# Chunked attention and a two-layer block on one core: direct first v, half-row scores, PSUM seeds, three more quarters by sevens, a written order

## The chip, the core and the metric

One core of a Trainium2 chip. The metric is device time in microseconds from the start to the end of one execution. The runs of the kernel before took 275.38, 275.7 and 276.49 us; their median, 275.7 us, is the time before. The profiled execution has its own time: its span, from the first to the last instruction, is 273.8 us. TensorE multiplies, VectorE and ScalarE work on tiles and take results out of PSUM (eight banks), GpSimd works on tiles and issues the loads, SyncE issues the transposing transfers and the stores.

## The reference

Attention inside chunks of 64 rows over q, k, v of 8 x 8 heads x 576 rows x 64, all float32:

```python
scores = scale * np.matmul(q_c, k_c.transpose(0, 1, 2, 4, 3))
scores = scores - np.max(scores, axis=-1, keepdims=True)
attn = np.exp(scores)
attn = attn / (np.sum(attn, axis=-1, keepdims=True) + 1e-09)
out = np.matmul(attn, v_c)
```

The result, with heads side by side, is x of 4608 tokens x 512. Two layers follow: `h = x @ w_in` (512 x 2048), `g = max(0.01 h, h)`, `g @ w_out` (2048 x 512), float32 out. The kernel works in float16 with sums in float32.

## The kernel before

**Groups.** Attention runs in 36 groups `u` of 128 tokens (two chunks of all eight heads). A group's steps, by the names they have in the program (`group`, line 865): `arrive` loads q and k (GpSimd's queue, converted to float16 on the way); `pe_t` transposes q and k on TensorE for u < 10 (`stage_tq`, `stage_tk`: the tiles qp and kp, four matmuls each), later groups by SyncE's transposing transfers `t`; `p` copies q into QZ (two copies, one for each half of the heads, into a tile whose other half is zero, so that one 128-row matmul gives two heads' scores); `k` copies kp to KT; `s` makes the scores in eight matmuls of 64 moving columns (`stage_s`, line 446, tile Sp); `m`, `b`, `x`, `z`, `n` are maximum, subtraction, exponential, sum with 1e-9 added and reciprocal, and scaling (tiles mx, sh, ex, z/ze/zi, en); `e` and `d2` transpose en on TensorE and copy it (tpe, et), or `d` does it by a transfer; `v` multiplies by v in eight matmuls (`stage_v`, tile xp), and `a` copies xp to xT, the input of the first layer.

**v.** v lies in VB as 128-row tiles whose two diagonal 64 x 64 blocks hold two heads and whose other blocks are zero (steps `zv`). From the second batch on, `load_v` (line 110) loads it straight into place in two transfers, one for each 64-row half. The first batch comes in five transfers of 128 token rows each into spare tiles (`load_v_rows`, line 124), and 18 copies on ScalarE, VectorE and GpSimd put it in place (`place_v`, line 129).

**Layers.** Tokens are cut into four blocks of 128 and eight of 512 (`BLOCKS`), j = 0 to 11. The first four, and blocks 4 and 5 in the first layer, are plain: `mm1` (tile hT) with 128 moving columns, `g` the leaky ReLU on ScalarE, `mm2` (oP), `out`, `save`. In blocks 6 to 11 a "quarter" of the first layer can be made by seven products in place of eight (`first_fast`, line 996, tiles hA, hB, hC; `FAST`, line 53, tells how many of the four quarters, `UNIT` whether the unit is 256 or 512 tokens). There, product 1 goes to PSUM bank A; a ScalarE copy `d` seeds bank B with it, product 2 adds to B; products 6, 7 and 4 add to A, with copies `u2` and `u3` taken between; 5 and 3 go to C; VectorE adds `+u3` and `+u2`; four leaky ReLUs finish it. The second layer of blocks 4 to 11 is made in the same way (`second_fast`, line 1055, tiles oA, oB, oC, fourteen half-products `m2` of eight matmuls with 256 columns), but there `d` copies product 1 to SBUF, product 2 opens bank B by itself, and VectorE adds the two into the output's C11 part. The sums of g that the products need are `sf`, those of x are `xf`, those of the weights `wf` and `vf`.

**Order.** All steps are put in a list with costs, and `run` (line 637) orders them: a list scheduler with a model of engines and load queues picks the next step, banks and spare tiles, with several hundred small adjustments in `TUNE` (line 776) and the engine of many steps in `ON` (line 820). Before a late step of the start it puts `idle` matmuls on the identity (line 532). Each engine executes its instructions in the order emitted, and so does each queue: GpSimd's carries all loads. The start's load order stands in `front` (line 826): q and k of group 1, k of 2, w_in's first quarter (Q0, two halves), the identity, q2, q3, v's first three pieces, k3, Q1, Q2, and so on; w_out comes in four parts P0 to P3.

Of the kernel before, what the change touches and what calls it, by code (L numbers as in the profile page):

```python
# [16 lines left out]
def kernel(  # L17
# [15 lines left out]
    CH = 64  # L33
# [19 lines left out]
    FAST = {6: 4, 7: 3, 8: 4, 9: 2, 10: 4, 11: 4}  # L53
    UNIT = {6: 256, 7: 256}
    POOL_N, POOL_X, POOL_S = 9, 20, 20
# [66 lines left out]
    V_T: dict[int, bass.AP] = {}  # L122

    def load_v_rows(n):
        r0, r1 = n * G, min((n + 1) * G, S)
        V_T[n] = sbp.tile([128, H, D], FP16, name="v_t", tag=f"tmp{(2 + n) % 6}", bufs=1)
        nc.gpsimd.dma_start(out=V_T[n][:r1 - r0], in_=v[0, :, r0:r1, :].rearrange("h p d -> p h d"))
# [67 lines left out]
    def leaky(to, of):  # L195
        nc.scalar.activation(out=to, in_=of, func=AFT.Prelu, bias=0.0, scale=1.0, alpha=0.01)  # L196

    def copy(to, of):
        nc.scalar.activation(out=to, in_=of, func=AFT.Copy, bias=0.0, scale=1.0)  # L199
# [23 lines left out]
    def evict2(j, ti):  # L223
        OSB[j, ti] = osb_tile()[:, 0]
        copy(OSB[j, ti], OP.pop((j, ti)))
# [52 lines left out]
    def x_form(j, h, i):  # L278
        (x11, x12), (x21, x22) = x_halves(j, h)
        f = x_sums(j, h)  # L280

        def less(to, a, b):
            (nc.gpsimd if j >= POOL_X else nc.vector).tensor_tensor(out=to, in0=a, in1=b, op=ALU.subtract)
# [53 lines left out]
    def g_form(j, i):  # L337
# [5 lines left out]
        if i == 0:  # L343
            plus(SF[j, 0], a21, a22)
        elif i == 1:
            minus(SF[j, 1], SF[j, 0], a11)
        elif i == 2:
            (nc.gpsimd if j >= POOL_S else nc.vector).tensor_tensor(out=a21, in0=a11, in1=a21, op=ALU.subtract)
        else:
            (nc.gpsimd if j >= POOL_S else nc.vector).tensor_tensor(out=a12, in0=a12, in1=SF[j, 1], op=ALU.subtract)  # L350

    def out_product(j, m, p, tag=None):
# [6 lines left out]
        }[m]  # L359
        if j == LAST:  # L360
            key = (j, p, "o" + IN[m])
            if m in OPENS:
                PA[key] = bank([128, HM], "o" + IN[m], tag)
            to, fresh = PA[key], m in OPENS
        else:
            key = (j, "o" + IN[m])
            if m in OPENS and p == 0:
                PA[key] = bank([128, 2, HM], "o" + IN[m], tag)
            to, fresh = PA[key][:, p, :], m in OPENS and p == 0
# [46 lines left out]
    def stage_k(u):  # L416
        KT[u] = sbp.tile([128, 4, 2, CH], FP16, name="KT", tag="KT", bufs=4)
        nc.scalar.activation(out=KT[u], in_=KP.pop(u), func=AFT.Copy, bias=0.0, scale=1.0)
# [27 lines left out]
    def stage_s(u, tag="Sp"):  # L446
        qz, kt = QZ[u % NQZ], KT.pop(u)
        Sp = psp.tile([128, 8, CH], FP32, name="Sp", tag=tag, bufs=1)
        for i in range(8):
# [19 lines left out]
    def stage_x(u):  # L469
        E[u] = sbp.tile([128, 8, CH], FP16, name="ex", tag="ex", bufs=2)  # L470
        nc.scalar.activation(out=E[u], in_=SH.pop(u), func=AFT.Exp, bias=0.0, scale=SCL)  # L471

    ZI: dict[int, bass.AP] = {}

    def stage_z(u):
        z = sbp.tile([128, 8], FP32, name="z", tag="z", bufs=2)
        nc.vector.tensor_reduce(out=z, in_=E[u], axis=AXL.X, op=ALU.add)  # L477
        ze = sbp.tile([128, 8], FP32, name="ze", tag="ze", bufs=2)
        nc.vector.tensor_scalar_add(out=ze, in0=z, scalar1=1e-9)
        ZI[u] = sbp.tile([128, 8], FP32, name="zi", tag="zi", bufs=2)  # L480
        nc.vector.reciprocal(out=ZI[u], in_=ze)  # L481
# [45 lines left out]
    def stage_a(u):  # L527
        xp = XP.pop(u)
        at = u * G % RING
        nc.scalar.activation(out=xT[:, :, at:at + G], in_=xp, func=AFT.Copy, bias=0.0, scale=1.0)  # L530
# [26 lines left out]
    class Hold:  # L557
# [3 lines left out]
        def fits(self, slots):  # L561
            return [y for y in slots if not self.written or y[1] in written]

    written: set = set()

    class Step:
# [12 lines left out]
    free: dict[str, list[tuple[float, object]]] = {  # L579
        "bank": [(0.0, x) for x in BANKS], "tmp": [(0.0, x) for x in range(NTMP)],  # L580
    }

    class Queues:

        def __init__(self):
            self.now, self.ring, self.out, self.n = 0.0, ([], []), ({}, {}), [0, 0]
            self.done, self.still = 0, []  # L590

        def matmuls(self, n, t):
            self.done += n
            if self.done >= 140:
                self.done -= 128
                if t > STALLS_FROM:
                    self.still.append((t + 0.75, t + 0.75 + STALL))

        def put(self, q, step, at, packets, slow):
            self.ring[q].append([at, packets, slow, step])  # L600
            self.n[q] += 1

        def heads(self):
            return [r[0] if r and r[0][0] <= self.now + 1e-9 else None for r in self.ring]

        def rates(self, h):
            if any(a - 1e-9 <= self.now < b - 1e-9 for a, b in self.still):
                return (0.0, 0.0)
            if h[0] and h[1]:
                return (370.0, 695.0 / h[1][2]) if h[1][2] > 1 else (425.0, 399.0)  # L610
            return (ALONE[0] if h[0] else 0.0, ALONE[1] / h[1][2] if h[1] else 0.0)

        def event(self):
            h = self.heads()
            v = self.rates(h)
            t = [self.now + x[1] / y for x, y in zip(h, v) if x and y]
            t += [r[0][0] for r, x in zip(self.ring, h) if r and not x]
            if any(h):
                self.still = [x for x in self.still if x[1] > self.now + 1e-9]
                t += [y for x in self.still for y in x if y > self.now + 1e-9]  # L620
            return min(t, default=None)

        def advance(self, to, landed):
            while self.now < to:
                e = self.event()
                t = to if e is None else min(e, to)
                h = self.heads()
                for x, y in zip(h, self.rates(h)):
                    if x:
                        x[1] -= (t - self.now) * y  # L630
                self.now = t
                for q, x in enumerate(h):
                    if x and x[1] < 1e-6:
                        self.ring[q].pop(0)
                        landed(q, x[3], t + (AFTER[q] if q == 0 or self.ring[0] else 2.0))

    def run():
        now = {e: 0.0 for e in LAT}
        now.update(pe=3.8, act=2.6, dve=0.95, pool=1.2, sp=1.3)
        left = {id(s): len(s.after) for s in steps}  # L640
        users: dict[int, list[Step]] = {}
        for s in steps:
            for x in s.after:
# [590 lines left out]
```

## Time and profile before

| | us |
|---|---|
| median of three runs (275.38 to 276.49) | 275.7 |
| span of the profiled execution | 273.8 |
| TensorE busy (PE), 96% of the span | 263.2 |
| weight loads (PEld, beside PE) | 238.2 |
| VectorE (DVE) | 208.2 |
| ScalarE (ACT) | 193.9 |
| GpSimd (POOL) | 158.9 |
| first matmul / first product of the first layer (hT) starts | 5.96 / 18.35 |

A row of the chain or of the view in order of time gives the start, the length, the engine, the line of the program, what is written from what, and a count. The length of a TensorE row runs to the last result; the distance to the next row's start is what the row costs the queue. In the stages, each pair is an engine's busy time and its instruction count. The granted TensorE clock is 1.00 in all stages.

### The profile page before, as it was taken

The page shows a single profiled execution, that of the slowest core. Times are in us where ns is not written, and L with a number is a line of the kernel's source. Part 1 is how long each engine was busy: PE and PEld are TensorE (multiplying, and loading weights), DVE is VectorE, ACT ScalarE, POOL GpSimd, SP SyncE. Part 2 cuts the span into 40 slices and gives each one's busy share as a digit, 9 for nine tenths or more (in the row PEclk, how much of TensorE's full clock was granted, in tenths as well). Part 3 has the DMA queues.
Part 4 walks back from the last instruction along what each step waited for, and adds up shares of the span by engine and source line. Part 5 has one row for each costly group of instructions (what it writes and reads, how often), then busy time and mean ns, then how long its engine had stood idle before and what let it go on. Part 6 is the DMA issues. An engine that isn't in the chain of part 4 may idle for free.

```text
span 273.8 us, 8229 instructions
## 1 busy us (share of the span) xinstructions
PE 263.2 (96%) x3406; PEld 238.2 (87%) x3406; DVE 208.2 (76%) x375; ACT 193.9 (71%) x359; POOL 158.9 (58%) x198
## 2 busy tenths in 40 slices
PE   1999999999999999999999999999999999999995
PEld 1889578799999999999999999899999989888884
DVE  5895285789978898899788999897879865831671
ACT  6588947778475644999796369978866896378721
POOL 8999783967898959587758778657351000000000
PEclk9999999999999999999999999999999999999999
DMA  9999999999999999999999999999954100220233
GB/s 134 154 191 183 182 176 176 155 173 217 151 158 152 120 143 208 170 144 234 154 155 121 136 140 247 133 186 197 136 84 151 43 19 2 77 79 0 79 115 116
DMA packets 162004, 38.27 MB, mean 140 GB/s; under 512 B 153008, under 2 KB 157616, under 8 KB 161968
## 3 DMA queue, kind: packets, MB, share of 16 engines
q0 software_dynamic: 114384, 18.09, 97.0%
q1 hardware_dynamic: 46544, 19.41, 42.2%
q8 instruction: 26, 0.43, 0.6%
q10 hardware_dynamic: 1040, 0.26, 0.4%
q14 instruction: 10, 0.08, 0.2%
HBM read 36.70 MB, written 9.44 MB: 169 GB/s over the span
## 4 chain that ended last, share of the span: by engine, by line
PE 90%; ACT 3%; DMA 3%; POOL 2%; issue 1%; DVE 0%; POOLq 0%
PE oA L371 20%; PE hT L185 17%; PE hA L323 14%; PE oC L371 10%; PE hC L323 7%; PE oP L210 5%; PE oB L371 5%; PE hB L323 3%; PE Sp L451 3%; PE xp L517 3%; DMA q_in<-in_q_dram 3%; PE tpe L495 1%; PE idle L535 1%; ACT gT L196 1%; ACT xT L530 1%; PE qp L404 1%
## 5 line engine op out<-in xcount | busy, mean ns | idle before, releaser
L371 PEld LDWEIGHTS <-gT 128*128 128x128 f16 x640 | 61.1, 98 | 6.6
L185 PE MATMUL hT<-xT,w_inT 128*128 128x128 f16 (+1 forms) x864 | 58.6, 225 | 0.1
L185 PEld LDWEIGHTS <-w_inT 128*128 128x128 f16 x864 | 53.1, 98 | 2.0 <-issue 0.4
L444 POOL COPY QZ<-QT 64x512 f16<-64x512 f16 x52 | 36.6, 705 | 20.0 <-DMA QT<-q_in 13.1
L196 ACT ACTIVATE gT<-hT 128x512 f16<-128x512 f32 x60 | 35.1, 599 | 15.9 <-PE hT L185 15.6
L235 DVE TENSOR_TENSOR tmp<-hC,tmp 128x512 f32<-128x512 f32 x42 | 27.9, 678 | 16.6 <-PE hC L323 8.3
L487 POOL TENSOR_TENSOR en<-ex,zi 128x512 f16<-128x512 f16 x22 | 23.8, 1083 | 26.8 <-DVE zi L481 12.3
L323 PEld LDWEIGHTS <-VF 128*128 128x128 f16 x448 | 34.5, 98 | 2.4
L93 POOL DMA_DIRECT2D q_in<-in_q_dram x39 | 33.8, 871 | 4.5 <-DMA w_outT<-in_moe_w_out_dram 1.8
L93 POOL DMA_DIRECT2D k_in<-in_k_dram x39 | 33.5, 863 | 1.2 <-DMA VB<-in_v_dram 0.8
L461 DVE TENSOR_REDUCE mx<-Sp 128x8 f32<-128x512 f32 x36 | 24.6, 684 | 10.3 <-PE Sp L451 10.2
L371 PE MATMUL oA<-WF,gT 128*128 128x256 f16 x256 | 32.2, 273 | 0.0
L199 ACT ACTIVATE tmp<-hA 128x512 f32<-128x512 f32 x42 | 24.3, 602 | 6.8 <-PE hA L323 6.8
L196 ACT ACTIVATE gT<-tmp 128x512 f16<-128x512 f32 x42 | 26.4, 634 | 3.7 <-DVE tmp L235 3.6
L323 PEld LDWEIGHTS <-w_inT 128*128 128x128 f16 x336 | 26.2, 98 | 1.9
L471 ACT ACTIVATE ex<-sh 128x512 f16<-128x512 f32 x36 | 22.8, 633 | 7.0 <-DVE sh L465 6.8
L371 PEld LDWEIGHTS <-S 128*128 128x128 f16 x256 | 24.6, 98 | 2.8
L477 DVE TENSOR_REDUCE z<-ex 128x8 f32<-128x512 f16 x36 | 24.3, 676 | 3.3 <-ACT ex L471 3.2
L530 ACT ACTIVATE xT<-xp 128x512 f16<-128x512 f32 x36 | 21.4, 597 | 7.6 <-PE xp L517 7.4
L465 DVE TENSOR_TENSOR sh<-Sp,mx 128x512 f32<-128x512 f32 x36 | 24.5, 681 | 0.6
L323 PE MATMUL hA<-XF,VF 128*128 128x128 f16 (+1 forms) x224 | 24.7, 246 | 0.0
L199 ACT ACTIVATE tmp<-oA 128x512 f32<-128x512 f32 (+1 forms) x27 | 14.9, 552 | 11.7 <-PE oA L371 11.6
(76 smaller groups left out, 478.7 us busy)
## 6 DMA issues: line engine op xcount, KB each, us to landing
out_dram<-osb SPq DMA_DIRECT2D x14, 512.0 KB, 5.2
VB<-in_v_dram POOLq DMA_DIRECT2D x14, 288.0 KB, 9.1
q_in<-in_q_dram POOLq DMA_DIRECT2D x31, 128.0 KB, 8.3
k_in<-in_k_dram POOLq DMA_DIRECT2D x31, 128.0 KB, 8.4
w_inT<-in_moe_w_in_dram POOLq DMA_DIRECT2D x8, 256.0 KB, 7.5
w_outT<-in_moe_w_out_dram POOLq DMA_DIRECT2D x4, 512.0 KB, 9.0
out_dram<-osb SPq DMA_DIRECT2D x6, 256.0 KB, 5.5
v_t<-in_v_dram POOLq DMA_DIRECT2D x4, 128.0 KB, 7.0
```

The costliest lines, as they stand in the source:

```text
L93: nc.gpsimd.dma_start(out=t[a - u * G:z - u * G], in_=src[b, :, r:r + z - a, :].rearrange("h p d -> p h d"))
L185: nc.tensor.matmul(out=hT[:, i, :], lhsT=w_inT[:, t, fc * 128:(fc + 1) * 128], rhs=xT[:, t, r0 % RING:r0 % RING + tb], start=(i == 0 and t ...
L196: nc.scalar.activation(out=to, in_=of, func=AFT.Prelu, bias=0.0, scale=1.0, alpha=0.01)
L199: nc.scalar.activation(out=to, in_=of, func=AFT.Copy, bias=0.0, scale=1.0)
L235: (nc.vector if e == "dve" else nc.gpsimd).tensor_tensor(out=to, in0=a, in1=b, op=ALU.add)
L323: nc.tensor.matmul(out=PA[key][:, c, :], lhsT=w[:, t, fc * 128:(fc + 1) * 128], rhs=x[:, t, :], start=(m in (1, 5) and c == 0 and t == 0), ...
L371: nc.tensor.matmul(out=to, lhsT=lhs[:, fc, p * 128:(p + 1) * 128], rhs=rhs[:, fc, :], start=(fresh and fc == 0), stop=(fc == HB - 1), skip ...
L444: nc.gpsimd.tensor_copy(out=QZ[u % NQZ][part, :, :, s, :], in_=QT[u][part].rearrange("p i (e t) -> p i e t", e=2))
L461: nc.vector.tensor_reduce(out=MX[u], in_=SP[u], axis=AXL.X, op=ALU.max)
L465: nc.vector.tensor_tensor(out=SH[u], in0=SP.pop(u), in1=MX.pop(u).unsqueeze(2).to_broadcast((128, 8, CH)), op=ALU.subtract)
L477: nc.vector.tensor_reduce(out=z, in_=E[u], axis=AXL.X, op=ALU.add)
L530: nc.scalar.activation(out=xT[:, :, at:at + G], in_=xp, func=AFT.Copy, bias=0.0, scale=1.0)
```

## The change

1. `load_v_rows` and `place_v` go; the first batch of v is loaded by `load_v`, straight in place, in four pieces of two or three chunks, two transfers each, and the load order of the start is another.
2. The scores of groups 0 to 3 (`SQ = 4`) are made by sixteen matmuls, each on one 64-row half, from an unpadded copy of q (one copy, `stage_q1`), not from QZ.
3. `second_fast`: `d` copies product 1 into PSUM bank B, product 2 adds to it, and the new step `c11` copies the sum out.
4. `FAST` is 4 in all six blocks: 24 quarters by sevens, not 21 (one more in block 7, two in block 9).
5. The sum's tail is cut in steps (`z`, `ze`, `zi`), and many steps may run on another engine (`ON`): 21 of the 36 `ze` on ScalarE, five of the `a`, and some copies and leaky ReLUs on VectorE; some `xf` and one `sf` on GpSimd.
6. The scheduler, its queue model and `TUNE` go. `ORDER` lists all 1459 steps by number, with the bank or spare tile of each and the number of idle matmuls before it.

```diff
-    FAST = {6: 4, 7: 3, 8: 4, 9: 2, 10: 4, 11: 4}
+    FAST = {6: 4, 7: 4, 8: 4, 9: 4, 10: 4, 11: 4}
...
+    SQ = 4
...
-    def place_v(c, m, e):
-        to = VB[0][m * CH:(m + 1) * CH, :, c, m * CH:(m + 1) * CH]
-        of = V_T[c // 2][c % 2 * CH:(c % 2 + 1) * CH, m * H // 2:(m + 1) * H // 2, :]
-        move(e, to, of)
...
+    def stage_q1(u, e):
+        QT[u] = sbp.tile([128, H // 2, 128], FP16, name="QT", tag="QT", bufs=4)
+        move(e, QT[u], QP.pop(u).rearrange("p i e t -> p i (e t)"))
...
+        if u < SQ:
+            qt = QT.pop(u)
+            for i in range(8):
+                g, e, m = i // 4, i // 2 % 2, i % 2
+                for s in range(2):
+                    half = slice(s * CH, (s + 1) * CH)
+                    nc.tensor.matmul(
+                        out=Sp[half, i, :], lhsT=qt[half, 2 * m + g, e * CH:(e + 1) * CH], rhs=kt[half, 2 * m + g, e, :],
+                        start=(i == 0), stop=True, skip_group_check=True,
+                    )
+            return
...
+        for i, fill, *slots in ORDER:
+            s = steps[i]
+            if fill:
+                idle(fill[0], BANKS[fill[1]])
+            for h, slot in zip(s.take, slots):
+                h.slot = BANKS[slot] if h.pool == "bank" else slot
             s.emit()
...
-        for what in "q1 k1 k2 Q0 I q2 q3 V0 V1 V2 k3 Q1 Q2 q5 V3 q4 P0 k5 P1 k4 q6 k7 V4 P2 k6 q7 Q3 v1 P3".split():
+        for what in "q1 k1 I V0:2 Q0 q2 k2 Q1 V2:4 q3 k3 Q2 V4:6 P0 q4 k4 P1 q5 k5 V6:9 Q3 P2 q6 k6 P3 q7 k7 v1".split():
...
-        d = cp("d", p1)
-        p2 = mm(2, [g(1, 0) + [p1[1]]] * 2)
+        d = []
+        for p in ps:
+            e, t = on(key + ("d", p), "act", act=us[0], dve=us[1])
+            def seed(p=p, e=e):
+                at = (j, p, "oB") if last else (j, "oB")
+                PA[at] = bank([128, HM] if last else [128, 2, HM], "oB", B1[p].slot)
+                copy(PA[at], psum("oA", p), e)
...
+        p2 = mm(2, [[y, p1[1]] + g(1, 0) for y in (d if last else d * 2)])
...
-        s11 = sum_of("d", 0, lo, [x + osb_free() for x in two(p2, d)], B1)
+        s11 = []
+        for p in ps:
+            e, t = on(key + ("c11", p), "act", act=us[0], dve=us[1])
...
```

The string in `front` gives the steps their numbers; `ORDER` says in which order they are issued. Its loads begin: second half of Q0, k1, the identity, q1, k2, q2, first half of Q1, v chunks 2 and 3 (first half), v chunks 0 and 1 (first half), first half of Q0, v chunks 0 and 1 (second half), q3, v chunks 2 and 3 (second half), second half of Q1, a zero fill, v chunks 4 and 5 (two halves), k3, a zero fill, Q2 (two halves). On TensorE it has 94 idle matmuls (86 before), the last six of them behind the first `v`; then `mm1` of block 0 (first quarter), `v` of group 1, `mm1` of block 0 (second quarter), q3's transposes, `mm1` of block 1 (second quarter), k3's transposes, `e` of group 2, `mm1` of block 1 (first quarter), `v` of group 2, `s` of group 3, `mm1` of block 0 (third quarter).

More of the change, by code (lines that the diff above doesn't have):

```diff
@@ L193, in mm1, with leaky, copy @@
         HT[j, a, h] = hT
[L195 to L199, printed above, removed]
+    def leaky(to, of, e="act"):
+        if e == "act":
+            nc.scalar.activation(out=to, in_=of, func=AFT.Prelu, bias=0.0, scale=1.0, alpha=0.01)
+        else:
+            nc.vector.scalar_tensor_tensor(out=to, in0=of, scalar=0.01, in1=of, op0=ALU.mult, op1=ALU.max)
+    def copy(to, of, e="act"):
+        move(e, to, of)
     def act1(j, a, h=0):
@@ L282, in less @@
         def less(to, a, b):
-            (nc.gpsimd if j >= POOL_X else nc.vector).tensor_tensor(out=to, in0=a, in1=b, op=ALU.subtract)
+            minus(to, a, b, e)
         if i == 0:
@@ L578 @@
     BANKS = ["mm0", "mm1", "mm2", "mm3", "qp", "kp", "ox", "Sp"]
[L579 to L635, printed above, removed]
@@ L836, in front @@
             elif what[0] == "V":
[L837 to L844 removed]
+                arrive_v(0, *n)
             elif what[0] == "Q":
@@ L960, in first_plain @@
             at = k0 + c / n
-            s = add(("mm1", j, a, h), "pe", 0.875, lambda j=j, a=a, h=h, hd=hd: mm1(j, a, h, hd.slot), x_of(j, h * tb, (h + 1) * tb) + gone(j) + [get(("Q", nf * a // 4, m)) for m in range(2)], key=at, take=[hd], spare=SPARE)
+            s = add(("mm1", j, a, h), "pe", 0.897 if tb == 128 else 0.873, lambda j=j, a=a, h=h, hd=hd: mm1(j, a, h, hd.slot), x_of(j, h * tb, (h + 1) * tb) + gone(j) + [get(("Q", nf * a // 4, m)) for m in range(2)], key=at, take=[hd], spare=SPARE)
             note(j, h * tb, (h + 1) * tb, ("mm1", j, a, h))
```

312 lines of the change are left out of this document (116 added, 196 removed), and 161 rows, old and new, of tables (ON, ORDER).

## The prediction

> **What bounds the kernel now.** I read the page's chain of waits first, then the busy time by stage, then the instructions in order of time on TensorE.
>
> ```profile
> span 273.8 us, 8229 instructions
> ...
> PE 90%; ACT 3%; DMA 3%; POOL 2%; issue 1%; DVE 0%; POOLq 0%
> ```
>
> Nine tenths of the chain that ended last is TensorE. The stages (span, then busy us and count of PE, PEld, DVE, ACT, POOL, the granted clock, DMA):
>
> ```profile
> 30.00:40.00 10.00, 10.00 (x116) 6.82 (x115) 4.99 (x11) 7.12 (x12) 7.91 (x10) 1.00 1.80 180
> ...
> 120.00:140.00 20.00, 20.00 (x318) 19.18 (x316) 17.50 (x36) 18.11 (x35) 14.02 (x17) 1.00 1.89 177
> ...
> 270.50:273.80 3.30, 0.00 (x0) 0.00 (x0) 0.38 (x1) 0.00 (x0) 0.00 (x0) 1.00 0.33 119
> ```
>
> From 30 us on PE is full, while ScalarE and VectorE come near it (18.1 and 17.5 of 20 us). So the time is a sum of three things: the start until the first product, the matmuls issued after it, and the tail after 270.5. A microsecond taken out of the middle elsewhere than on PE is worth nothing; one more matmul costs its issue interval. Those intervals, from the long pieces of the chain (start, length, line, count):
>
> ```profile
> 54.09 4.47 PE hT L185 x80
> ...
> 158.06 0.87 PE hA L323 x8
> ```
>
> 4.47/80 = 0.0558 us for 128 moving columns, 0.87/8 = 0.109 us for 256.
>
> **The start.** TensorE in order of time (start, duration to the last result, count), then ScalarE:
>
> ```profile
> 13.12 0.40 PE L404 MATMUL qp<-ident,q_in 128*128 128x128 f16 x4 [0.35 <-DMA q_in<-in_q_dram]
> ...
> 17.25 0.40 PE L517 MATMUL xp<-et,VB 128*128 128x64 f16 x8
> ...
> 18.35 2.17 PE L185 MATMUL hT<-xT,w_inT 128*128 128x128 f16 x32
> 20.36 0.40 PE L451 MATMUL Sp<-KT,QZ 128*128 128x64 f16 x8
> 20.60 1.06 PE L185 MATMUL hT<-xT,w_inT 128*128 128x128 f16 x16
> ...
> 21.71 1.06 PE L185 MATMUL hT<-xT,w_inT 128*128 128x128 f16 x16
> 22.83 0.39 PE L517 MATMUL xp<-et,VB 128*128 128x64 f16 x8
> ...
> 27.08 1.06 PE L185 MATMUL hT<-xT,w_inT 128*128 128x128 f16 x16
> 28.39 0.40 PE L495 MATMUL tpe<-ident,en 128*128 128x128 f16 x4 [0.26 <-ACT gT L196]
> ```
>
> ```profile
> 14.77 2.45 ACT L118 ACTIVATE VB<-v_t 64x256 f16<-64x256 f16 x6
> 17.69 0.60 ACT L530 ACTIVATE xT<-xp 128x512 f16<-128x512 f32 x1 [0.46 <-PE xp L517]
> ```
>
> The first product starts at 18.35, 1.10 us after the first xp at 17.25 (0.44 until ScalarE starts xT, 0.60 for xT, 0.06). ScalarE copies v from 14.77 to 17.22, and the first xp stands right behind. After 18.35 three holes remain, read from start to start: 2.01 less 32 x 0.0558, 1.12 and 1.31 less 16 x 0.0558 each, or 0.22 + 0.23 + 0.42 = 0.87 us. After 28.4 there is nothing to win on PE but matmuls.
>
> How fast the loads come, from the tile views of w_in (three halves in a row) and of v (two 64-row halves in a row):
>
> ```profile
> L135 POOL DMA_DIRECT2D w_inT<-in_moe_w_in_dram x3: 612/615/654, 12.6 to 14.2; - x3
> ...
> DMA to landing us min/median/max: 7.2/7.7/8.2
> ```
>
> ```profile
> L111 POOL DMA_DIRECT2D VB<-in_v_dram x2: 1186/1187/1188, 33.3 to 34.4; - x2
> ...
> DMA to landing us min/median/max: 9.3/9.8/10.3
> ```
>
> The w_in halves land from 19.8 to 22.4 (14.2 + 8.2), 1.3 us apart. The v halves land at 42.6 and 44.7, 2.1 us apart for 2304 rows of 64, so 0.47 us for 512 rows.
>
> **The change, part by part.** (a) *Start.* The eighteen copies that place v go. The first xp now needs eight loads landed: one half of w_in, k1, q1, k2, q2, another w_in half, one v piece for chunks 2 and 3, the two v pieces for chunks 0 and 1, and a w_in half between those two. Three estimates of it:
> - By the load queue. In the kernel before, q2 landed just before 13.12, behind q1, k1, k2 and both halves of w_in's first quarter. Now one more w_in half (1.3) and three v pieces (3 x 0.47) precede the last piece: 13.1 + 1.3 + 1.4 = 15.8, and 1.10 later, 16.9, the first product.
> - By GpSimd's issue, which now runs past four w_in halves, six q or k loads, six v pieces, the identity and two zero fills before the last zero fill that the first xp needs:
>
> ```profile
> L196 ACT ACTIVATE gT<-hT 128x512 f16<-128x512 f32 x60 | 35.1, 599 | 15.9 <-PE hT L185 15.6
> L235 DVE TENSOR_TENSOR tmp<-hC,tmp 128x512 f32<-128x512 f32 x42 | 27.9, 678 | 16.6 <-PE hC L323 8.3
> ...
> L93 POOL DMA_DIRECT2D q_in<-in_q_dram x39 | 33.8, 871 | 4.5 <-DMA w_outT<-in_moe_w_out_dram 1.8
> ```
>
>   4 x 0.62 + 6 x 0.87 + 6 x 0.75 (a 512-row piece has no row; 0.62 and 0.87 bound it) + three small ones of 0.6 make 14.0 us; from about 1.2 that is 15.2, and the product 16.3 (15.5 to 17.0).
> - By VectorE: one copy of q instead of two, and the chain max, subtract, sum, scale at 0.68 each for the first group, give en about half a microsecond earlier than now; with nothing between en and xp but the transpose and one copy, 15.7.
>
> The latest of the three counts, but the queue's is padded by a slow first w_in; I take **16.5**, so **-1.85** (15.7 to 17.3: -2.65 to -1.05). (b) *Holes after it.* The queue brings the second half of w_in's third quarter at 22.4 as before, since the same loads stand ahead of it; the second quarter's is one k (0.87), two v pieces and two w_in halves earlier, 18.1. The written order wants them at 16.5 + 0.89 + 0.23 = 17.6 and, four products (3.6), five small steps (5 x 0.22) and the 64-row scores (0.46) after the first, 21.7; the first wait pushes the second. 0.6 us is lost against 0.87: **-0.27** (0 to 0.9 lost: -0.9 to 0). (c) *Work moved behind the first product.* Two sets of four transposes (2 x 0.22) and one xp (0.23) that PE did while it waited now come later: **+0.67**. (d) *Scores by halves.* Eight matmuls took 0.24 (20.36 to 20.60); sixteen take 0.23 more. No row shows one on a 64-row half; below, at nothing, if both halves run side by side; above, 0.47 in all. Three of the four groups lie in the wait for v, under filler matmuls; the fourth is on the path: **+0.23** (0 to +0.3).
>
> (e) *Three more quarters by sevens.* A plain quarter is 32 matmuls of 256 columns, 3.49 us. By sevens it is 28 of them, 3.05, in the block of 512-column units (two quarters), and 56 of 128 columns, 3.12, in the other (one): -0.44 x 2 - 0.37 = **-1.24**. This is only a count. Each puts three more instructions on ScalarE (seven for four) and two on VectorE, 3 x 3 x 0.60 and 3 x 2 x 0.68: 5.4 and 4.1 us in stages with 1.9 and 2.5 us free of 20. What hides them: copies that the list of engines moves between the two, the place copies gone, 21 of the 36 small additions of 1e-9 now on ScalarE. (f) *C11 in PSUM.* In eight blocks a copy to SBUF and an addition become a copy into PSUM and a copy out: the same number. New is the wait: product 2 starts after the seed is copied; by the xp and xT rows that takes 0.21 (17.25 + 0.23 to 17.69) + 0.60 + 0.06 = 0.87 us after product 1's last matmul is issued. Behind it on PE queues everything, as PE takes its order. The written order puts at least 1.5 us of other products between (blocks 6 and 8; the others 2 us or more), and in the last block four half-products, 3.5 us. Uncovered, it would be 8 x 0.87 = 7.0 us. I put (e)'s and (f)'s small stalls, and those of the rest of the written order, at **+0.2** (0 to +1.5). (g) *Tail.* The last store is now 256 KB after a ScalarE copy, not 128 KB after an addition; from the DMA view of the end:
>
> ```profile
> out_dram<-osb SPq DMA_DIRECT2D x2, 256.0 KB, 2.0
> out_dram<-osb SPq DMA_DIRECT2D x2, 128.0 KB, 1.7
> ```
>
> **+0.3** (0 to +0.5).
>
> Sum: -1.85 - 0.27 + 0.67 + 0.23 - 1.24 + 0.2 + 0.3 = **-1.96**; span 273.8 to 271.8. The runs' median 275.7 lies 1.9 above the span, which I keep: **273.7 us**. All low ends together (-4.1) give 271.6, and need the third w_in quarter before 22.4 too; all high ends (+0.7) give 276.4, and as the stalls and the late start need not meet I take 271.6 to 275.5 as this case's own range.
>
> **Rivals.** *Half rate for v.* A 64-row piece could take as long as 1024 rows on all partitions, 0.87 instead of 0.47. Three pieces ahead of the first xp make 1.2 later, six ahead of the third w_in quarter 2.4: the first product at 17.7, the 22.4 becomes 24.8, wanted at 22.9; in all 1.2 + 1.9 - 0.6 = 2.5 more: 276.2. The two v rows above speak against it. The Trainium skill's page "SBUF — State Buffer", section "Door 1: The DMA port swizzle", says 64 adjacent partitions reach only 8 of 16 ports and get about half the bandwidth of 128; by it alone the sum is this rival's. The trace does not agree for rows this short: 0.47 us for 512 of them, against 0.87 for a 1024-row issue's whole slot. 10 in 100.
>
> *Sevens without their gain*: the change doesn't do what it says, and the three quarters give back on waits for copies what PE saves: 1.24 more, 274.9. For it: ScalarE at 18.1 of 20 in the stage 120 to 140. Against: PE is full in that same stage with quarters by sevens in it. 10 in 100.
>
> *Slower: the quarters' chain of copies.* A quarter by sevens has three places where PE waits for a copy of the product before. If in each of the 24 quarters one copy comes half an instruction late (0.3 us) because ScalarE or VectorE, fuller by 5.4 and 4.1 us, is at another, 24 x 0.3 = 7.2 more: 280.9. It turns the sign against the forecast's 1.96 from 0.08 us a quarter, and beyond the noise from 0.14. Against it: 21 such quarters run today without a hole. 12 in 100.
>
> **How the numbers follow.** Forecast 61 in 100; the rivals 10, 10 and 12; 7 for a start earlier than 15.7 with no hole, under 271.6. About 0.5% (1.4 us) is what a measurement of this kernel can tell from no change, so faster means under 274.3. Of the forecast's 61, 50 lie there; with the 7 and 3 of the second rival that is 60. Slower is the third rival, 12. Same is the rest, 28. The range 271.5 to 276.5 leaves out the third rival and little else.
>
> **What would show it.** Right: the first hT near 16.5 with no copies of v on any engine; holes of about 0.6 us between it and 22.5, none over 0.2 later; no plain product of 256 columns left (12 today, 96 matmuls); the last matmul near 268. Wrong: an xp that waits for a DMA of VB past 16.5 (half rate); holes before the products hA, hC or oB with a ScalarE copy as releaser (the copies' chain). A first product after 18 or holes of over 2 us after 30 would make the prediction wrong.

## The result, and the profile after

The changed kernel takes 302.7 us (median of four runs, 299.6 to 303.8), the kernel before 276.1 beside it: 1.094 times as long, with a 95% interval from 1.085 to 1.103. The forecast was 273.7, its range 271.5 to 276.5; the kernel became slower by an amount that no rival covers. Ratios, here and below, leave out runs more than 1.5% above the quickest run of their kernel.

The page of the changed kernel (span; TensorE's granted clock and the transfers in 40 slices, in tenths; the load queue's packets, MB and share; the chain of waits; the loads of v, with the KB of each and the median time to landing), and two lines of the page of the kernel before:

```profile
span 302.1 us, 8361 instructions
...
PEclk9985579999999999999979999999999999999999
DMA  9999999999999999999999999999992420030043
...
q0 software_dynamic: 128256, 19.86, 105.3%
...
PE 70%; DMA 23%; POOL 3%; issue 1%; SPq 0%; ACT 0%; POOLq 0%
...
VB<-in_v_dram POOLq DMA_DIRECT2D x22, 288.0 KB, 9.9
```

```profile
DMA  9999999999999999999999999999954100220233
...
q0 software_dynamic: 114384, 18.09, 97.0%
```

TensorE's share of the chain fell from 90% to 70%, and the transfers' rose from 3% to 23%. The load queue moved 13,872 packets more. And all 22 loads of v have 288 KB: the eight "pieces" of the first batch too, each of which should have had 64 or 96. The reason is the body of `load_v`, which the change does not touch:

```python
    def load_v(b, m, c0, c1):
        nc.gpsimd.dma_start(
            out=VB[b % NVB][m * CH:(m + 1) * CH, :, :, m * CH:(m + 1) * CH].rearrange("p h c d -> p (h c) d"),
            in_=v[b, m * H // 2:(m + 1) * H // 2].rearrange("h (c j) d -> j (h c) d", j=CH),
        )
```

`c0` and `c1` do not occur in it. Every piece loads the whole 64-row half of the batch, 2304 rows, into the same place: eight transfers instead of two, 6 x 2304 = 13,824 rows too many, which is the packets' difference up to 48. And as all four of a half write one place, each waits until the one before it has landed. GpSimd in order of time (the bracket: how long it stood before, and for what), then TensorE:

```profile
6.75 1.20 POOL L114 DMA_DIRECT2D VB<-in_v_dram  x1
14.85 1.15 POOL L114 DMA_DIRECT2D VB<-in_v_dram  x1 [6.90 <-DMA VB<-in_v_dram]
15.98 0.64 POOL L126 DMA_DIRECT2D w_inT<-in_moe_w_in_dram  x1
16.59 1.19 POOL L114 DMA_DIRECT2D VB<-in_v_dram  x1
...
24.22 1.15 POOL L114 DMA_DIRECT2D VB<-in_v_dram  x1 [5.56 <-DMA VB<-in_v_dram]
...
31.21 1.15 POOL L114 DMA_DIRECT2D VB<-in_v_dram  x1 [3.53 <-DMA VB<-in_v_dram]
```

```profile
14.88 1.33 PE L564 MATMUL idle<-ident 128*128 128x128 f16 x21
36.31 0.59 PE L546 MATMUL xp<-et,VB 128*128 128x64 f16 x8 [20.09 <-DMA VB<-in_v_dram]
...
37.97 1.91 PE L176 MATMUL hT<-xT,w_inT 128*128 128x128 f16 x16
```

Behind the waiting GpSimd stand all other loads, w_in's and w_out's too. The first xp is emitted after six of the eight pieces, so it waits for all six. Everything else that it needs was as early as forecast: `et` was copied by 15.7, and the filler of 21 idle matmuls starts at 14.88 and takes 21 x 0.0558 = 1.2, so TensorE stood ready at 16.1, then idle for 20.1 us. The first product starts at 37.97, not 16.5.

The whole difference, in four parts, all worked out from TensorE's matmuls in order of time: the start of the first product; after it the matmuls, each at its issue interval (0.0558 for 128 moving columns, 0.109 for 256, in proportion for the others); what the distances from start to start exceed these by, called holes; and what follows the start of the last matmul.

| us | before | forecast | after | e1 (below) |
|---|---|---|---|---|
| first product starts | 18.35 | 16.5 | 37.97 | 16.72 |
| matmuls from there on | 249.86 | 249.52 | 249.52 | 249.52 |
| holes among them | 1.93 | 1.86 | 9.26 | 4.48 |
| from the last matmul's start to the end | 3.64 | 3.94 | 5.31 | 5.06 |
| span | 273.8 | 271.8 | 302.1 | 275.8 |

Of the 28.3 us, 19.6 are the start, 7.3 the holes, 1.7 the tail, less 0.3 in the matmuls. That the matmuls are as forecast says only that their number is: both columns price them at the forecast's own intervals. Part of the holes is the clock, in the stages after the stall (span, busy us of PE, PEld, DVE, ACT and POOL, the granted clock, transfers):

```profile
20.00:30.00 10.00, 0.00 (x0) 0.00 (x0) 0.00 (x0) 0.00 (x0) 3.47 (x4) 0.55 1.38 106
30.00:40.00 10.00, 3.63 (x40) 3.50 (x41) 1.68 (x5) 1.11 (x2) 8.42 (x12) 0.50 1.63 136
40.00:50.00 10.00, 10.00 (x177) 9.67 (x175) 4.09 (x9) 6.26 (x13) 5.69 (x7) 0.93 1.64 169
```

With TensorE idle from 16.2 the granted clock is 1.00 until 21.0, then 0.50 until 41.5, 3.5 us behind the start of the first product, and the first sixteen products take 1.91 us instead of 1.06. The Trainium skill's page "TensorE: Matmul & The Clock Gate", section "Part 1: The HAM clock gate", says that the array falls to half its clock after an idle window of about 3.4 us and gets it back after a busy one; this trace agrees. It shows more: the 7 in the PEclk row is a second fall to 0.50, from 154.1 to 157.5, right behind a wait of TensorE of only 2.2 us (151.6 to 153.8). So a stretch need not be idle throughout to cost the clock. In the two stretches at half clock that have work in them, 3.5 and 3.4 us long, the matmuls exceed their intervals by 1.7 us each: together 3.4 of the 9.26 us of holes.

### The profile page after: what moved, and what is told of

It is laid out like the page before. It is cut to its first block, busy times and chain, and to the rows that moved or that the text cites. A ratio compares the mean times of both kernels' runs of the same rounds, so it can differ in the third digit from the quotient of the medians.

```text
span 302.1 us, 8361 instructions
## 1 busy us (share of the span) xinstructions
PE 268.5 (89%) x3462; PEld 241.5 (80%) x3462; DVE 213.2 (71%) x368; ACT 181.5 (60%) x355; POOL 171.8 (57%) x205
## 4 chain that ended last, share of the span: by engine, by line
PE 70%; DMA 23%; POOL 3%; issue 1%; SPq 0%; ACT 0%; POOLq 0%
PE oA L366 15%; PE hA L317 13%; PE hT L176 12%; DMA VB<-in_v_dram 11%; PE oC L366 8%; PE hC L317 6%; PE oB L366 4%; DMA w_inT<-in_moe_w_in_dram 3%; DMA QT<-q_in 3%; PE hB L317 3%; DMA et<-en 3%; PE xp L546 3%; DMA out_dram<-osb 2%; PE Sp L462 2%; PE oP L204 2%
## 5 line engine op out<-in xcount | busy, mean ns | idle before, releaser
L176 PE MATMUL hT<-xT,w_inT 128*128 128x128 f16 x768 | 49.6, 222 | 0.2 <-DMA w_inT<-in_moe_w_in_dram 0.2
L176 PEld LDWEIGHTS <-w_inT 128*128 128x128 f16 x768 | 45.6, 100 | 1.3 <-issue 0.7
L317 PEld LDWEIGHTS <-VF 128*128 128x128 f16 x512 | 40.3, 98 | 3.0
L121 ACT ACTIVATE xT<-xp 128x512 f16<-128x512 f32 x31 | 18.4, 596 | 40.0 <-PE xp L546 40.0
L114 POOL DMA_DIRECT2D VB<-in_v_dram x22 | 25.7, 1176 | 20.9 <-DMA VB<-in_v_dram 16.0
L229 DVE TENSOR_TENSOR tmp<-hC,tmp 128x512 f32<-128x512 f32 x48 | 32.3, 684 | 6.9 <-PE hC L317 3.4
L472 DVE TENSOR_REDUCE mx<-Sp 128x8 f32<-128x512 f32 x36 | 24.6, 683 | 15.2 <-PE Sp L462 13.4
L546 PE MATMUL xp<-et,VB 128*128 128x64 f16 x288 | 14.9, 198 | 21.4 <-DMA VB<-in_v_dram 20.1
L121 ACT ACTIVATE tmp<-hA 128x512 f32<-128x512 f32 x46 | 26.4, 596 | 11.3 <-PE hA L317 10.5
L188 ACT ACTIVATE gT<-hT 128x512 f16<-128x512 f32 x48 | 27.0, 599 | 9.4 <-PE hT L176 9.1
L317 PEld LDWEIGHTS <-w_inT 128*128 128x128 f16 x384 | 30.7, 99 | 2.3
L546 PEld LDWEIGHTS <-VB 128*128 128x128 f16 x288 | 13.0, 101 | 22.9 <-issue 21.1
L317 PE MATMUL hA<-XF,VF 128*128 128x128 f16 (+1 forms) x256 | 27.5, 246 | 0.0
```

Of the source, the lines that this page charges most:

```text
L114: nc.gpsimd.dma_start(out=VB[b % NVB][m * CH:(m + 1) * CH, :, :, m * CH:(m + 1) * CH].rearrange("p h c d -> p (h c) d"), in_=v[b, m * H // ...
L176: nc.tensor.matmul(out=hT[:, i, :], lhsT=w_inT[:, t, fc * 128:(fc + 1) * 128], rhs=xT[:, t, r0 % RING:r0 % RING + tb], start=(i == 0 and t ...
L229: (nc.vector if e == "dve" else nc.gpsimd).tensor_tensor(out=to, in0=a, in1=b, op=ALU.add)
L317: nc.tensor.matmul(out=PA[key][:, c, :], lhsT=w[:, t, fc * 128:(fc + 1) * 128], rhs=x[:, t, :], start=(m in (1, 5) and c == 0 and t == 0), ...
L472: nc.vector.tensor_reduce(out=MX[u], in_=SP[u], axis=AXL.X, op=ALU.max)
L546: nc.tensor.matmul(out=xp[:, t, e, :], lhsT=VB[b % NVB][:, t, c, :], rhs=et[:, t // 2, e, t % 2, :], start=(e == 0 and t == 0), stop=True, ...
```

## The experiments

Twelve kernels, each beside the kernel before on the same chip. The first product's start and the holes are of the profiled run, read as in the table above. That is one run of several: in e1 and e6 it lies 2.3 and 3.7 us under the median, so small differences in the last column prove little.

| kernel | median us | ratio to before, 95% | first product | holes |
|---|---|---|---|---|
| after | 302.7 | 1.085 to 1.103 | 37.97 | 9.3 |
| e1 true pieces | 279.9 | 1.005 to 1.022 | 16.72 | 4.5 |
| e2 loaded once | 281.9 | 1.013 to 1.028 | 18.22 | 7.5 |
| e3 waits, few bytes | 291.7 | 1.048 to 1.063 | 26.86 | 7.7 |
| e4 bytes, own places | 290.5 | 1.044 to 1.059 | 20.55 | 13.5 |
| e5 before, 24 quarters | 280.8 | 1.001 to 1.029 | 17.96 | 6.6 |
| e6 as e1 | 280.4 | 1.002 to 1.015 | 16.69 | 3.8 |
| e7 no fifth batch of v | 278.2 | 0.999 to 1.009 | 16.68 | 5.6 |
| e8 a transfer a chunk | 287.8 | 1.029 to 1.056 | 20.69 | 10.4 |
| e9 one transpose earlier | 279.4 | 1.006 to 1.015 | 16.61 | 6.3 |
| e10 e8 mended | 287.2 | 1.028 to 1.050 | 17.68 | 12.6 |
| e11 no stores of block 4 | 276.3 | 0.990 to 1.001 | 17.20 | 3.7 |
| e12 e11, e7 and e9 | 275.5 | 0.989 to 0.998 | 16.86 | 2.9 |

### Is it the repeated load? e1 and e2

e1 lets each piece load its own chunks. For a part of the chunks, heads and chunks no longer merge into one stride as they do in `load_v` for all nine, so VB is kept chunk by chunk, and rows of v change places:

```diff
-    VB = [sbp.tile([128, H // 2, NCH, 128], ...
+    VB = [sbp.tile([128, NCH, H // 2, 128], ...
...
+        rows = v[b, m * H // 2:(m + 1) * H // 2].rearrange("h (c j) d -> j (h c) d", j=CH)
-            out=VB[b % NVB][m * CH:(m + 1) * CH, :, :, m * CH:(m + 1) * CH].rearrange("p h c d -> p (h c) d"),
+            out=VB[b % NVB][m * CH:(m + 1) * CH, c0:c1, :, m * CH:(m + 1) * CH].rearrange("p c h d -> p (c h) d"),
+            in_=rows[:, 4 * c0:4 * c1, :],
```

> The changed kernel with each of the first batch's eight v transfers cut to its own chunks (512 rows, 768 for the last pair). For this VB is kept chunk by chunk, and of the first two batches which v rows land where is permuted (the output is not the reference's); the number of transfers, their places in the order and all other work stay. Repeated whole loads are the cause: the first hT product comes near 16.5 us, the GpSimd waits on VB are gone, and the time is my old sum, 273.7 us (272 to 276). Half rate for transfers of 64 partitions: first hT after 18 us, about 276.2. The written order, the seeds or the other engines cost the time by themselves: above 290 us, with the later holes still there.

e2 issues the two whole halves once, early, and v stays where it was:

```diff
+        if b == 0:
+            m = {2: 0, 0: 1}.get(c0) if m == 0 else None
+            if m is None:
+                return
```

> The changed kernel with the first batch of v loaded once: the two whole halves (2304 rows each) in the first two places of the eight, nothing in the other six; output as the reference's. Repeated loads are the cause: first half lands at 14.6 us as now, the second 3.3 us later near 17.9, w_in's first half behind it near 19.2, so first hT near 19.5 to 20 and the time 3 us above my old sum, 276 to 278. The written order by itself: above 290 us.

TensorE in e1, in order of time, and e1's loads of v:

```profile
15.64 0.39 PE L547 MATMUL xp<-et,VB 128*128 128x64 f16 x8
...
16.72 1.05 PE L177 MATMUL hT<-xT,w_inT 128*128 128x128 f16 x16
...
21.52 0.44 PE L456 MATMUL Sp<-KT,QT 64*64 64x64 f16 x16
21.89 1.29 PE L177 MATMUL hT<-xT,w_inT 128*128 128x128 f16 x20
```

```profile
VB<-in_v_dram POOLq DMA_DIRECT2D x6, 64.0 KB, 5.5
VB<-in_v_dram POOLq DMA_DIRECT2D x2, 96.0 KB, 9.8
```

The repeated load is the cause of the great loss: with true pieces the ratio falls from 1.094 to 1.014, and in e2, with the same order, seeds, engines and quarters, to 1.021. The start is the forecast's, 16.72 for 16.5. That excludes half rate for v (17.7), and so do the landings: pieces issued in a row land 0.42 to 0.43 us apart (12.31 and 12.74, 17.59 and 18.01) where the forecast took 0.47. But e1 is not at 273.7: it is slower than before. That is taken up below, after the two prices. e2 missed its expectation both ways: its start, 18.22, is earlier than 19.5 to 20, and its 281.9 us lie above 276 to 278. Of its 7.5 us of holes 5.7 lie between 115 and 135 us, where e1 has 1.6.

### Waits or bytes? e3 and e4

e3: the pieces overlap by a chunk (0:3, 2:4, 3:6, 5:9), so GpSimd still waits for landings. e4: whole halves, but those of 2:4 and 4:6 into WF, those of 6:9 into the second batch's tile; no two first-batch loads write one place.

```diff
+        a = {0: 0, 2: 2, 4: 3, 6: 5}[c0] if b == 0 else 0
+        c1 = 3 if c1 == 2 else c1
```

```diff
+        if b == 0 and c0 in (2, 4):
+            flat = WF.rearrange("p a b c -> p (a b c)")[m * CH:(m + 1) * CH, 2304 * (c0 // 4):2304 * (c0 // 4 + 1)]
+            to = flat.rearrange("p (x d) -> p x d", d=D)
+        if b == 0 and c0 == 6:
+            to = VB[1][...]
```

> As e1, but each of the first batch's pieces also covers a chunk of a piece issued before it (0:3, 2:4, 3:6, 5:9), so that the chain of waits of GpSimd on earlier landings stays with a third more rows instead of four times as many; permuted rows as in e1. If the waits are the larger price: three or four waits of some 2 us issue to landing each in GpSimd's order, first hT beyond 22 us and the time over 285. If the bytes are: first hT 17.5 to 20, time 275 to 279.

> The changed kernel with all eight whole-half loads, but only the 0:2 pair goes to the first batch's place; 2:4 and 4:6 go to the tile of w_out's formed sums (written later), 6:9 to the second batch's tile. The bytes stay, the waits of one v transfer on another go. If the bytes are the larger price: v's second half lands near 22.5, first hT near 24, w_in's third block near 37, time 285 to 292. If the waits are: first hT under 21 and the time under 281. If both, the two runs e3 and e4 together leave a rest of the 29 us that neither shows.

Beyond e1, the waits cost 1.0557 - 1.0136 = 4.2% of the time before, the bytes 1.0515 - 1.0136 = 3.8%; together 8.0%, and from e1 to the changed kernel it is 1.0936 - 1.0136 = 8.0%. So each is about half of it (11.6 and 10.5 us of 276). e3 came out as its first alternative; of e4's, the start fits "waits" and the time "bytes". That the two add up to the whole is in part chance. Each ratio is known to about 0.8%; e3 also loads a third more rows than e1, and GpSimd stands 9.6 us for v in it against 16.0 in the changed kernel; and the parts do not add up: the starts are 10.1 and 3.8 us later than e1's, together 13.9 for 21.3, and the holes 3.2 and 9.0 larger, together 12.2 for 4.8. GpSimd in e3, and TensorE's waits of e3 (us in total, times, longest):

```profile
12.80 0.75 POOL L117 DMA_DIRECT2D VB<-in_v_dram  x1 [5.19 <-DMA VB<-in_v_dram]
...
20.21 0.69 POOL L117 DMA_DIRECT2D VB<-in_v_dram  x1 [4.40 <-DMA VB<-in_v_dram]
```

```profile
PE xp L549 <- POOL VB L587: 9.5, 1, 9.5
```

The first xp waited there not for v, but for a zero fill of VB that stands in GpSimd's order behind the waits. In e4 no load of v holds GpSimd for another, and the start is only 3.8 us later than e1's, but the loads behind are late, with holes of their own (TensorE, in order of time):

```profile
19.47 0.39 PE L552 MATMUL xp<-et,VB 128*128 128x64 f16 x8 [3.14 <-DMA VB<-in_v_dram]
23.29 1.89 PE L182 MATMUL hT<-xT,w_inT 128*128 128x128 f16 x16 [0.86 <-DMA w_inT<-in_moe_w_in_dram]
28.06 0.40 PE L410 MATMUL kp<-ident,k_in 128*128 128x128 f16 x4 [0.75 <-DMA k_in<-in_k_dram]
```

GpSimd is not free in e4 either: its seven loads from 19.66 to 28.30 us each begin only when the load eight places ahead has landed, and it stands 5.4 us for that. The same holds in all fourteen traces: no load of GpSimd's begins before the one eight places ahead of it has landed, and the nearest comes 0.28 us behind. Whether the program or the chip sets that limit, no run here shows. The clock has its part too: in e4 it is 0.50 from 21.0 to 27.9.

The row of the transfers in the page of before is at 9 for the first 29 of 40 slices, until about 199 us. That hints that a load more would be paid, and e4 bears it out: 13,824 rows more cost 10.5 us, where the prediction's 2.1 us for 2304 rows makes 12.6. The prediction read TensorE's rows and passed over that one.

### The quarters alone: e5

The kernel before with its planner, and `FAST` at 4 in all blocks.

> The kernel before with one of the change's parts alone: 24 instead of 21 quarters by sevens (blocks 7 and 9 too); the order comes from the planner as before, v is loaded as before. My term for it: 1.24 us less, 274.4 beside 275.7. If the quarters' chain of copies stalls TensorE (my slower rival): 277 to 281. If the gain is eaten by a later wait for transposes or loads, because the transfers are busy at 90% or more until 200 us in this kernel too: 275.5 to 276.5, with a new hole of about 1 us between 80 and 140 us.

The count is right: priced at the forecast's intervals, the matmuls after the first product fall from 249.86 to 248.62, the forecast's 1.24. And still it is no faster, at 1.015 times (1.001 to 1.029): the holes grow from 1.9 to 6.6, all the new ones between 155 and 190 us. TensorE's waits:

```profile
PE hA L323 <- DVE XF L283: 1.7, 1, 1.7
PE oC L371 <- ACT xT L530: 0.9, 1, 0.9
PE hB L323 <- ACT hB L199: 0.7, 1, 0.7
```

VectorE comes late with the sums of x, and ScalarE with copies: near the mechanism of the slower rival, in the planner's order. In the written order (e1, e6, after) none of these rows is among TensorE's waits, and in e1 TensorE is busy for all of 150 to 195 us. So the planner's order loses the quarters' gain there, and the written one does not. My third guess there, a wait for transfers, missed.

### Why e1 is not at 273.7: e6, e7, e9, e11, e12

e1's sum lacks 4 us: holes 4.48 for 1.86, tail 5.06 for 3.94, start 0.2. By the ratio it lacks 5.8 (1.014 for 0.993 of 275.7); the rest is in no trace, as the profiled run lies under the median. Of the holes, 1.2 lie between 20 and 40 us (the load of w_out below), 1.1 between 80 and 100, 1.6 between 120 and 140. TensorE's waits in e1:

```profile
PE Sp L463 <- POOL QZ L444: 1.6, 2, 1.3
PE oP L205 <- DMA w_outT<-in_moe_w_out_dram: 1.0, 1, 1.0
```

The scores of group 22 wait near 127 us for GpSimd's copies of q. The same hole stands in the changed kernel (2.2 us of waiting) and, at 1.3 us or more, in every run with this order and block 4's stores, except e9 and e10, which move a transpose. In e6, GpSimd and TensorE there:

```profile
127.40 0.61 POOL L444 COPY QZ<-QT 64x512 f16<-64x512 f16 x1 [3.75 <-DMA QT<-q_in]
```

```profile
128.73 0.41 PE L463 MATMUL Sp<-KT,QZ 128*128 128x64 f16 x8 [1.32 <-POOL QZ L444]
```

So the transposed q is late. Four runs asked why: without the fifth batch's v loads (e7: `load_v` returns for b = 4), with the transpose of q's group 22 two places earlier in SyncE's order (e9), without the two stores of block 4 ahead of it (e11; 256 rows or 512 KB each, which its expectation puts at 256 KB), and with all three (e12).

```diff
-  ... (784, 0), ... (801, 0), ... (798, 0), ...
+  ... (798, 0), (784, 0), ... (801, 0), ...
```

```diff
     def save_side(j, side):
+        if j == 4:
+            OSB.pop((j, side))
+            return
```

> The kernel of e1 once more, on the same chip as e7 and e8, as their base: 277.5 to 281 us.

> The kernel of e6 without the loads of the fifth batch of v (two whole halves, issued at 103.6 and 104.7 us in e1; the batch's chunks are then those of the batch that stood in the tile before). If the hole at 127.8 us (scores waiting for q's copies, these for the transposed q, 9.7 us from issue to landing) comes from the transfers' backlog: it is gone or under 0.3 us, and the time is 1.5 to 2.5 us below e6. If it comes from the written order (GpSimd or SyncE come to the transpose too late by their own programs): the hole stays within 0.5 us of e6's, and the time with it.

> The kernel of e1 with one step of the written order moved: SyncE issues the transpose of q's group 22 before the two transposes of k's groups 21 and 22, not after them (permuted v rows as in e1). If SyncE's order makes the hole near 127 us: q's transpose goes out some 4 us earlier and the hole (1.5 to 2.8 us in the runs so far) is under 0.5 us, the time 1 to 2.5 us below e1 and e6, 275 to 278. If the transposes' backlog makes it: the hole moves to the scores of group 21, and the time stays at 278 to 281.

> The kernel of e1 without the two 256 KB stores of block 4 (issued at 110.1 and 110.7 us, landed at 118.8 and 120.8 in e1; 512 rows of the output are not written), which stand in SyncE's order ahead of the transposes that are late near 127 us. If they hold the transposes up: the hole at 127 us is under 0.5 us and the time 1 to 2.5 us below e1 and e6. If the transposes are late by their own number: the hole stays at 1.3 to 2.8 us.

> The kernel of e11 with, besides, the fifth batch's v loads left out (as e7) and the transpose of q's group 22 moved ahead (as e9). The holes between 115 and 135 us are 2.0 us together in e6 and 3.6 in e9. If other traffic makes the transposes late: under 0.5 us together. If the order asks for the scores and products of groups 17 to 22 sooner than SyncE can issue and land their transposes (some 1.3 to 2.5 us to issue one, 8 to 10 us to land): still 1.5 us or more.

e7: the hole stays (2.4 us of waiting at its longest); v's loads alone do not make it. Against e6 on the same chip the intervals overlap (0.999 to 1.009, 1.002 to 1.015), so no gain is shown. e9: the hole moves, as the second theory said, to the xp's around it and to scores that wait for a transposed k, and the time stays (1.011):

```profile
PE xp L547 <- DMA et<-en: 2.2, 3, 1.2
PE Sp L463 <- DMA KT<-k_in: 0.8, 1, 0.8
```

e11: the hole falls to 0.7 us of waiting, but not because the scores come sooner. They start at 129.17 us, in e1 at 129.43 and in e6 at 128.73; TensorE, held up before (a start of 17.20, 2.1 us of waits for q), came there at 128.5, in e6 at 127.4. The ratio falls to 0.996, clear of e6's interval, but the profiled spans, 274.9 and 275.0, and the holes, 3.7 and 3.8, do not show where. e12: the hole is gone, TensorE's waits name no transposed tile at all, and the holes between 115 and 135 us are 0.7 together, a little over the 0.5 expected, most of it one wait for GpSimd's sums of x. The ratio is 0.994 (0.989 to 0.998). That the forecast's 273.7/275.7 is 0.993 is chance: e12 leaves work out, its start, holes and tail are all longer than forecast, and its profiled span is 273.7 beside 273.8 before. The transposes between 100 and 130 us, with the median time to landing, in e6 and in e12:

```profile
QT<-q_in SPq DMA_TRANSPOSE x5, 8.8
et<-en SPq DMA_TRANSPOSE x4, 8.9
KT<-k_in SPq DMA_TRANSPOSE x4, 9.1
```

```profile
QT<-q_in SPq DMA_TRANSPOSE x5, 6.0
et<-en SPq DMA_TRANSPOSE x5, 5.5
...
KT<-k_in SPq DMA_TRANSPOSE x4, 4.9
```

So without v's loads and the two stores of 512 KB, and with the one transpose moved, a transpose takes 5 or 6 us and not 9. Neither alone does that: by the same view, in the order of the rows above, the medians are 8.2, 9.1 and 9.1 in e7, 8.5, 9.0 and 8.6 in e11, and 9.1, 9.4 and 9.7 in e9. Nor do slow transposes alone make the hole: in the kernel before they take 7.9, 7.5 and 8.7 in that stretch, with four stores and four loads of v, and TensorE waits for none. So the traffic alone does not make the hole; a written order that asks for the tile too soon after its transpose belongs to it. How much each of the three steps of e12 gives is open. The Trainium skill's page "DMA: Bandwidth & Descriptors", section "Issuing engines are not separate DMA queues", says that transfers of all issuing engines run on the same 16 DMA engines and interleave; e12 fits, where SyncE's transposes are shorter without GpSimd's loads and SyncE's stores. e11 and e12 leave work out, so their time is no gain that a whole kernel has; that it can be had by moving the stores was not tried.

### True pieces in v's own layout: e8 and e10

```diff
+        if b == 0:
+            for c in range(c0, c1):
+                nc.gpsimd.dma_start(
+                    out=VB[0][m * CH:(m + 1) * CH, :, c, m * CH:(m + 1) * CH],
+                    in_=v[0, m * H // 2:(m + 1) * H // 2, c * CH:(c + 1) * CH].rearrange("h j d -> j h d"),
+                )
+            return
```

> The changed kernel with the first batch's v loaded truly piece by piece and in the reference's layout: one transfer for each chunk and half (256 rows), 18 instead of 8, in the same places of the order; output as the reference's. GpSimd then issues two transfers where e6 issues one, 0.7 us more each, four of them before the first xp can run. If GpSimd's issue sets the start: first hT near 17.5 to 18.5 and 1 to 2 us above e6. If the transfers themselves do: first hT within 0.5 us of 16.7 and the time within 1 us of e6.

> The kernel of e8 (correct v, a transfer for each chunk and half) with three moves: chunks 0 and 1 of both halves first, two zero fills of VB from GpSimd to ScalarE near 4 us (in e8 the first xp waited 3.2 us for one of them, behind the issues), and the transpose of e9. If e8's loss is that fill behind the issues: first hT at 16.5 to 17.5 and 276 to 279. If it is the number of transfers: first hT past 18.5, above 281.

Neither expectation of e8 held: the first product came at 20.69, since the first xp waited 3.2 us for a zero fill behind GpSimd's issues. e10 took that away and started at 17.68, just past the 16.5 to 17.5 expected, but was no faster: ten more issues (four take 2.5 us in e8) put off the loads behind them, and TensorE paid later. The half of w_in that it waits for first was issued at 18.5, in e1 at 15.8 (TensorE in e10, in order of time):

```profile
25.51 6.03 PE L184 MATMUL hT<-xT,w_inT 128*128 128x128 f16 x80 [2.60 <-DMA w_inT<-in_moe_w_in_dram]
...
46.45 0.40 PE L407 MATMUL qp<-ident,q_in 128*128 128x128 f16 x4 [2.47 <-DMA q_in<-in_q_dram]
```

So the number of issues counts there, as the second theory of e10 said, though by another place than the first product. The limit of eight loads counts loads too, not rows: e8's GpSimd stands 1.1 us at 11.2 for the load eight places ahead. No kernel with the whole computation beat the one before; of the repairs, e2 is the best.

## Why the prediction was wrong, point by point

**The step that failed** is (a), in its words "three v pieces (3 x 0.47)", and with it the list of what the first xp needs ("one v piece for chunks 2 and 3, the two v pieces for chunks 0 and 1"). They took from the call and from the names in `front` that a piece loads its chunks. The body of `load_v` does not use them, so a piece was 2304 rows and not 512, it waited for the one before it, and the xp needed six and not two. The first product came 21.5 us later than forecast, which is three quarters of the error of 29 us; e1, e3 and e4 show the rest of it, holes and clock, to hang on the same loads but for what e1 itself lacks, 4 us in its trace and 5.8 by its ratio. It was there to be read before: the diff leaves `load_v` as it is, and the v row that the prediction priced by the piece (2.1 us for 2304 rows) was the row of every call. That the change might not do what it says was weighed for the quarters alone.

**The rest of (a)** holds when the pieces are pieces: 16.72 in e1. Of the three estimates GpSimd's was the near one: the zero fill that the first xp needs ends at 15.21 in e1, for 15.2, and in e9 the xp waits 0.46 us for it. The load queue's was late: the last piece that the xp needs landed at 14.47, not 15.8, so the latest of the three did not count.

**(c), (d) and (e)** together: -0.34 forecast, 249.52 - 249.86 = -0.34 by the matmuls in the traces of after and e1, at the forecast's intervals; so the count is confirmed, not the price. By itself (e) is -1.24 in e5's matmuls, in the same sense. (d) is smaller than taken: sixteen half-row scores take 21.89 - 21.52 = 0.37, 0.13 more than eight took (taken 0.23, bounds 0 to 0.3).

**(b)** came out better than taken: e1 has next to no hole between its first product and 30 us, where 0.6 was to be lost. The last half of w_in's third quarter landed at 21.41, not 22.4.

**(e)'s and (f)'s stalls and the rest of the written order**, mis-sized: put at 0.2 with a bound of 1.5. With (b), the holes were to fall by 0.07 and rose by 2.55 in e1 and 1.89 in e6. The seeds are no part of it: no wait of TensorE in e1 is for oB. What was not seen is the rest of the order: w_out's load near 30 us and the transposes near 127 us. The waits are shown; that traffic and order together make the one near 127 is what e12 and the kernel before point to, and the share of each is open.

**(g)**, mis-sized: +0.3 forecast, +1.4 in e1, +1.7 after. The stores of 256 KB at the end, in e1, by the view that gave 2.0 before:

```profile
out_dram<-osb SPq DMA_DIRECT2D x2, 256.0 KB, 2.4
```

The 2.4 is the median of two. The last store takes 2.8 from issue to landing (271.44 to 274.24), against 1.7 for the last of the kernel before, which is 1.1 of the 1.4; the other 0.3 stands between that landing and the end, 1.5 for 1.2. Why this store takes 2.8 in e1, 3.1 after and 2.0 in e11 is open.

**The rivals.** *Half rate*: excluded by e1's start and landings. *Sevens without their gain* and *the quarters' chain of copies*: not seen in the written order; in the planner's (e5) the gain is lost to late sums and copies, 4.7 us of holes and not 7.2. **The signs** named in advance did their work: a first product after 18, an xp that waits for a DMA of VB, and holes of over 2 us after 30 all stand in the trace; only the reading "half rate" that was put beside the second was wrong.

## What to carry to other kernels

Read the body of a helper whose call gets new arguments before pricing the call, and check it on the first profile by the KB and packets of its transfers: a repeated load shows there at once, and transfers into one place wait for each other and hold up everything behind them in their queue. Where the transfers' row stands at 9, reckon that a load more is paid (here 10.5 us of an estimated 12.6), and leave a transpose, in an order written out by hand, the time that it takes among stores and loads. When a hole shrinks, look whether the awaited work came sooner or the engine came later (e11). A count of matmuls is a good forecast of TensorE's work and a poor one of the time, as e5 shows with 1.24 us fewer matmuls and a longer run.

## What was not expected of the hardware

A transposing transfer took 5 to 6 us from issue to landing with two loads and two stores less around it, and 9 with them; leaving out the loads alone or the stores alone left it at 8 to 9. No load of GpSimd's began before the one eight places ahead had landed, in any trace. Idle for 20 us, TensorE came back at a granted clock of 0.50, and its first sixteen products took 1.91 us instead of 1.06. A wait of 2.2 us at 151.6 was followed by 3.4 us at 0.50 as well; in e7 one of 2.4 us was not. Sixteen score matmuls on 64 rows took 0.37 us where eight on 128 rows took 0.24: less than twice the time for twice the number.
